# Start addresses of the first layer's moving buffers, chosen per chunk, in a fused attention and feed-forward kernel

## The chip, the core and the metric

The kernel runs on one core of one Trainium2 chip. The metric is the device time of one execution in microseconds (us). Three executions of the kernel before took 633.62, 634.3 and 634.36 us; the median is 634.3 us.

## What is computed

Block-sparse attention is followed by a two-layer feed-forward network. Attention has 4 batches, 8 heads, 768 positions and a head dimension of 64; each query sees its neighbours within 16 positions and one summary of every block of 32 keys. The output becomes a matrix x of 3072 rows by 512 columns, and the network takes it from there:

```python
a = softmax(concat([masked local scores, summary scores + log(32)]))
x = (a @ concat([v, v_sum])).transpose(0, 2, 1, 3).reshape(3072, 512)
h = np.maximum(x @ w_in, 0.0)        # w_in: 512 x 2048
out = (h * h) @ w_out                # w_out: 2048 x 512
```

## The kernel before, in words

The 3072 rows are handled as 24 groups of 128 rows; two groups make a chunk of 256 rows, so there are 12 chunks, numbered 0 to 11. The 2048 hidden columns are 16 slices of 128, called f.

**Two parts for each number.** Every float32 operand of the feed-forward part is split in a high part, rounded to the narrower format that TensorE multiplies in one pass (float32r), and a low part that holds the rest. A product is then three matmuls: high weights by high data, low weights by high data, high weights by low data. For the attention output the two parts are `xh` (written by ScalarE, L375) and `xl` (written by VectorE, L378). For the weights they are `w_sb[f][:, 0]` and `w_sb[f][:, 1]`. For the squared hidden values they are `gh` (L405) and `gl` (L413).

**First layer** (`ffn1`, L387 to L395). For one chunk and one f there are 12 matmuls at L391: for each of 4 slices of the 512 columns the three products above. The weights (128x128) are the stationary operand, loaded anew for each matmul; `xh` or `xl` (128x256) is the moving operand that streams through.

**Second layer** (`ffn2`, L425 to L436). For one chunk and one f there are 6 matmuls at L432. Here `gh` or `gl` (128x128) is the stationary operand and the weights (128x512) are the moving one.

**Order.** The start, chunks 0 and 1, follows a list written out by hand (`START`), while weights are loaded and split. Chunks 2 to 11 then run in a loop over pairs of slices (`slot`): 24 matmuls of the first layer, then the 12 of the second layer for the pair before, and between them the attention work of the chunk after next. A chunk has 8 such slots. At the end of its eighth slot the attention outputs of the next chunk are computed (L361), split into `xh` and `xl`, and the scores of a later one (L278) are taken; TensorE does this between two chunks. All engines take their instructions in the order in which the kernel writes them.

**Buffers.** `x_part` (L368 to L372) hands out the buffer of a chunk: two buffers each for `xh` and `xl`, used in turn, taken from the pool `work`. Each is 4096 bytes long in every partition: 4 slices of 256 float32 numbers, so each slice begins 1024 bytes after the one before. In the program as built all four begin 352 bytes past a multiple of 512. All weights `w_sb` and both `gh` and `gl` begin 160 bytes past a multiple of 512, and the pieces that a matmul takes of them lie at whole multiples of 512 from there. So, counted in bytes modulo 512, the moving operand lies 192 bytes past the stationary one in every matmul of the first layer, and 0 bytes past it in every matmul of the second layer.

Of the kernel before, what the change touches and what calls it, by code (L numbers as in the profile page):

```python
# [12 lines left out]
F32R = mybir.dt.float32r  # L13
# [11 lines left out]
P = 128  # L25
NT = S // P
NPAIR = H // 2
TPC = 2
CT = TPC * P
# [44 lines left out]
def attn_ffn_kernel(ctx: ExitStack, tc: tile.TileContext, q, k, k0, kt, v, vt, v0, w, masks, gmasks, ident, mean, out):  # L74
# [3 lines left out]
    const = ctx.enter_context(tc.tile_pool(name="const", bufs=1))  # L78
    big = ctx.enter_context(tc.tile_pool(name="big", bufs=1))
    work = ctx.enter_context(tc.tile_pool(name="work", bufs=2))  # L80
# [25 lines left out]
    pT = [const.tile([P, H, P], F32, name=f"pT{i}") for i in range(2)]  # L106
    ksum = const.tile([P, NPAIR, NB], F32, name="ksum")
    vsum = const.tile([P, NPAIR, 32], F32, name="vsum")
    r_sb = const.tile([P, 2, CT], F32, name="r")
    gh_sb = const.tile([P, 4, CT], F32R, name="gh")  # L110
    gl_sb = const.tile([P, 4, CT], F32R, name="gl")
# [138 lines left out]
    xh, xl = {}, {}  # L250
# [117 lines left out]
    def x_part(x, name, g):  # L368
        c, o = divmod(g, TPC)
        if c not in x:  # L370
            x[c] = work.tile([P, NPAIR, CT], F32R, name=name, tag=name)
        return x[c][:, :, o * P : (o + 1) * P]  # L372

    def high_x(g):
        nc.scalar.copy(out=x_part(xh, "xh", g), in_=x_ps[g])  # L375

    def low_x(g):
        nc.vector.tensor_sub(out=x_part(xl, "xl", g), in0=x_ps.pop(g), in1=x_part(xh, "xh", g).bitcast(F32))  # L378
# [244 lines left out]
    with tc.manual_schedule(engines=None):  # L623
        for token in START.split():
            what, i, j, eng = re.fullmatch(r"(L:[a-z]+|F[12]|[A-Z]+)\.?(\d*)\.?(\d*)([avp]?)", token).groups()
            i, j = int(i or 0), int(j or 0)
# [10 lines left out]
        for c in range(2, n_c):  # L637
            for f in range(0, NF, 2):
                n = (f + 2) // 2 % 8
# [85 lines left out]
```

## Time and profile before

| what | value |
|---|---|
| median of three executions | 634.3 us (633.62 to 634.36) |
| the profiled execution, its own time | 633.53 us |
| its span, first to last instruction | 631.7 us |
| mean granted TensorE clock | 0.986 |
| TensorE matmuls busy (PE) | 601.6 us, 95% of the span |
| weight loads busy (PEld) | 545.1 us, 86% |
| VectorE (DVE), ScalarE (ACT), GpSimd (POOL) busy | 385.4, 262.5 and 88.8 us |

Such a profile is of one execution. PE is TensorE's matmuls and PEld its weight loads, which overlap them. The recorded duration of one matmul runs from its issue to its modelled end and overlaps that of the next; how fast a stream of matmuls really runs is read from the distance between their starts. The timeline gives, row by row, the start in us, the duration of the merged instructions, the engine, the line, the tiles written and read, and how many were merged.

### The profile page before, as it was taken

Reading aid. Unit: us, or ns where it says so; the run is one execution under the profiler, and the core shown is the slowest. Engines: PE = TensorE matmul, PEld = TensorE weight load, DVE = VectorE, ACT = ScalarE, POOL = GpSimd, SP = SyncE. Lnnn points to the kernel's source line nnn. Section 1 sums busy time; section 2 is a strip of 40 time slices with the busy share of each in tenths; the row PEclk is TensorE's granted clock in tenths of the full one; section 3 lists DMA queues with packets and bytes.
Section 4 is the critical chain, followed back from the end, with each engine's and each line's share of the span. In section 5 each row is a group of like instructions: output and inputs, shape, how many; then the busy total and the mean of one; then the engine's idle time right before and its main releaser. Section 6 shows DMA issues by size and latency. Waiting matters only on the chain.

```text
span 631.7 us, 14142 instructions
## 1 busy us (share of the span) xinstructions
PE 601.6 (95%) x5792; PEld 545.1 (86%) x5792; DVE 385.4 (61%) x1077; ACT 262.5 (42%) x690; POOL 88.8 (14%) x83
## 2 busy tenths in 40 slices
PE   3689999999989999999999998999999999999997
PEld 2588889989979999999989988998998998998996
DVE  4889888668535755756644772783763663653221
ACT  3778887332424324424424423334433423332222
POOL 2555663002000000002000000000200000000000
PEclk9879999999999999999999998999999999999999
DMA  8999611553043134123026115205005001000000
GB/s 290 381 341 317 212 71 52 166 164 90 1 111 110 49 87 132 51 76 93 1 58 162 51 38 148 84 1 135 35 1 135 34 0 52 34 2 1 34 1 33
DMA packets 55104, 60.56 MB, mean 96 GB/s; under 512 B 40320, under 2 KB 40448, under 8 KB 52992
## 3 DMA queue, kind: packets, MB, share of 16 engines
q1 hardware_dynamic: 55040, 59.67, 31.5%
q8 instruction: 45, 0.74, 0.5%
q14 instruction: 19, 0.16, 0.1%
HBM read 53.36 MB, written 6.29 MB: 94 GB/s over the span
## 4 chain that ended last, share of the span: by engine, by line
PE 91%; DMA 4%; DVE 2%; issue 1%; SPq 1%; ACT 0%; DVEq 0%
PE ph L391 41%; PE o_ps L432 41%; DMA w_raw<-in_w 4%; PE ph L361 3%; PE s_ps L391 3%; PE s_ps L278 2%; DVE w_raw L236 1%; PE s_ps L361 1%; PE ph L336 0%; PE s_ps L293 0%; PE s_ps L261 0%; DVE w_sb L247 0%; SPq L171 0%; DVE sm L323 0%; ACT w_raw L225 0%
## 5 line engine op out<-in xcount | busy, mean ns | idle before, releaser
L391 PE MATMUL ph<-xh,w_sb 128*128 128x256 f32 x1448 | 264.2, 284 | 2.8 <-issue 2.2
L391 PEld LDWEIGHTS ph<-xh,w_sb 128*128 128x128 f32 x1448 | 228.9, 190 | 10.7 <-issue 2.4
L432 PE MATMUL o_ps<-w_sb,gh 128*128 128x512 f32 x768 | 237.2, 390 | 0.0
L391 PE MATMUL ph<-xl,w_sb 128*128 128x256 f32 x724 | 204.6, 283 | 0.0
L410 DVE TENSOR_TENSOR ph<-ph,r 128x512 f32<-128x512 f32 (+1 forms) x101 | 64.9, 643 | 160.5 <-ACT r L399 159.2
L432 PEld LDWEIGHTS o_ps<-w_sb,gh 128*128 128x128 f32 x768 | 137.3, 188 | 22.8 <-issue 0.2
L432 PE MATMUL o_ps<-w_sb,gl 128*128 128x512 f32 x384 | 149.7, 390 | 0.9 <-DVE gl L413 0.9
L399 ACT ACTIVATE r<-ph 128x512 f32<-128x512 f32 (+1 forms) x91 | 52.0, 571 | 226.0 <-PE ph L391 225.1
L391 PEld LDWEIGHTS ph<-xl,w_sb 128*128 128x128 f32 x724 | 140.1, 194 | 0.0
L314 ACT ACTIVATE e_sb<-e_sb,nmx 128x88 f32<-128x88 f32 (+1 forms) x192 | 69.9, 367 | 71.3 <-DVE nmx L306 71.3
L347 DVE STREAM_TRANSPOSE pT<-e_sb 32x256 f32<-32x256 f32 x216 | 94.1, 436 | 3.4 <-POOL e_sb L330 0.4
L432 PEld LDWEIGHTS o_ps<-w_sb,gl 128*128 128x128 f32 x384 | 72.1, 188 | 16.4 <-DVE gl L413 1.3
L330 POOL TENSOR_TENSOR e_sb<-e_sb,sm 128x352 f32<-128x352 f32 (+1 forms) x43 | 34.7, 810 | 336.4 <-DVE sm L324 198.4
L413 DVE TENSOR_TENSOR gl<-ph,gh 128x512 fp32r<-128x512 f32 (+1 forms) x101 | 64.3, 637 | 10.5 <-DVE ph L410 0.5
L405 ACT ACTIVATE gh<-r 128x512 fp32r<-128x512 f32 (+1 forms) x112 | 64.0, 571 | 9.3 <-DVE r L401 5.8
L240 POOL TENSOR_TENSOR w_raw<-w_raw 128x1024 int32<-128x1024 int32 x16 | 35.6, 2233 | 25.4 <-DVE w_raw L236 8.7
L314 ACT ACTIVATION_READ_ACCUMULATOR e_sb<-e_sb,nmx 128x1 f32 x192 | 36.4, 190 | 0.0
L306 DVE CUSTOM_DVE_ANT_0 e_sb<-s_ps,gmask_sb 128x88 f32<-128x88 f32 x144 | 27.1, 244 | 0.4
L378 DVE TENSOR_TENSOR xl<-ph,xh 128x512 fp32r<-128x512 f32 x19 | 13.1, 691 | 22.4 <-ACT xh L375 22.4
L323 DVE TENSOR_SCALAR sm<-sm 128x4 f32<-128x4 f32 x48 | 13.4, 280 | 16.0 <-ACT e_sb L314 16.0
L375 ACT CAST xh<-ph 128x512 fp32r<-128x512 f32 x19 | 11.1, 587 | 26.6 <-PE ph L361 26.6
L361 PEld LDWEIGHTS ph<-pT,v_sb 128*64 128x64 f32 x608 | 18.6, 138 | 3.8 <-issue 3.2
(66 smaller groups left out, 391.3 us busy)
## 6 DMA issues: line engine op xcount, KB each, us to landing
w_raw<-in_w SPq DMA_DIRECT2D x16, 1024.0 KB, 14.9
v_sb<-in_v SPq DMA_DIRECT2D x24, 384.0 KB, 4.9
kv<-in_kt SPq DMA_DIRECT2D x16, 384.0 KB, 3.4
q_sb<-in_q SPq DMA_DIRECT2D x24, 256.0 KB, 5.3
out<-ob SPq DMA_DIRECT2D x24, 256.0 KB, 2.1
k_sb<-in_k SPq DMA_DIRECT2D x18, 256.0 KB, 5.1
kv<-in_vt SPq DMA_DIRECT2D x12, 384.0 KB, 3.9
k_sb<-in_k SPq DMA_DIRECT2D x18, 128.0 KB, 5.2
```

Of the source, the lines that this page charges most:

```text
L240: nc.gpsimd.tensor_tensor(out=hi, in0=hi, in1=lo, op=ALU.add)
L306: nc.vector.tensor_tensor_reduce(out=e_sb[:, h, 0:n], in0=s_ps[g][h % 2][:, h // 2, 0:n], in1=m, scale=-scale, scalar=3.0e38, op0=ALU.add, ...
L314: nc.scalar.activation(e, e, AF.Exp, bias=nmx[half][:, i : i + 1], scale=-1.0, accum_out=sm[half][:, i : i + 1])
L330: eng.tensor_mul(out=e, in0=e, in1=sm[half].unsqueeze(2).to_broadcast([P, 4, n]))
L347: nc.vector.transpose(out=pT[g % 2][j * 32 : j * 32 + 32, :, i * 32 : i * 32 + 32], in_=e_sb[i * 32 : i * 32 + 32, :, c : c + 32],)
L361: nc.tensor.matmul(xp[o : o + 64, h // 2, s * 64 : s * 64 + 64], lhsT=v_sb[g % 2][:, s, h * 64 : h * 64 + 64], rhs=pT[g % 2][:, h, s * 64 ...
L391: nc.tensor.matmul(ph, lhsT=w_sb[f][:, w, cc * P : (cc + 1) * P], rhs=x[c][:, cc, :], start=(n == 0), stop=(n == 3 * NC4 - 1))
L399: nc.scalar.activation(r, ph, AF.Relu)
L405: nc.scalar.activation(gh, r, AF.Square)
L410: nc.vector.tensor_mul(out=ph, in0=ph, in1=r)
L413: nc.vector.tensor_sub(out=gl, in0=ph, in1=gh.bitcast(F32))
L432: nc.tensor.matmul(o_ps[c][tt], lhsT=g_[:, ts_], rhs=w_sb[f][:, w, DM:], start=(first and n == 0), stop=(last and n == 2),)
```

## The change

The buffers of `xh` and `xl` are no longer taken from the pool. Four buffers (two for each, used in turn as before) are allocated once, 512 bytes longer than needed. For each chunk a table gives where in its buffer `xh` and `xl` begin, in bytes:

```diff
+    begin_x = [(0, 0), (0, 0), (0, 0), (64, 64), (128, 128), (192, 192), (256, 256), (32, 32), (0, 64), (0, 128), (0, 256), (320, 320)]
+    x_buf = {n: [const.tile([P, NPAIR * CT + 128], F32R, name=f"{n}{i}") for i in range(2)] for n in ("xh", "xl")}
...
         if c not in x:
-            x[c] = work.tile([P, NPAIR, CT], F32R, name=name, tag=name)
+            o_ = begin_x[c % len(begin_x)][0 if name == "xh" else 1] // 4
+            x[c] = x_buf[name][c % 2][:, o_ : o_ + NPAIR * CT].rearrange("p (a k) -> p a k", a=NPAIR)
         return x[c][:, :, o * P : (o + 1) * P]
```

In the program as built the new buffers begin 160 bytes past a multiple of 512, as the weights do, so the table's numbers are the distances of the moving operand from the weights, modulo 512. Before, that distance was 192 in every chunk; now it is 0 in chunks 0 to 2, 192 in chunk 5 alone, and another number in each of the others; in chunks 8 to 10 `xh` is at 0 and `xl` at 64, 128 and 256. The buffers of `r`, `gh`, `gl` and the weights lie 18432 bytes (36 times 512) further on than before, so their places modulo 512, and with them the second layer's distance of 0, are as they were. The instructions of every engine, their order and the semaphore values that they wait for are the same in both programs; the addresses alone differ.

## The prediction

> **What bounds the kernel now.** I read the page of the profile first: the busy times, then the chain that ended last.
>
> ```profile
> PE 601.6 (95%) x5792; PEld 545.1 (86%) x5792; DVE 385.4 (61%) x1077; ACT 262.5 (42%) x690; POOL 88.8 (14%) x83
> PE 91%; DMA 4%; DVE 2%; issue 1%; SPq 1%; ACT 0%; DVEq 0%
> L391 PE MATMUL ph<-xh,w_sb 128*128 128x256 f32 x1448 | 264.2, 284 | 2.8 <-issue 2.2
> L391 PE MATMUL ph<-xl,w_sb 128*128 128x256 f32 x724 | 204.6, 283 | 0.0
> L432 PE MATMUL o_ps<-w_sb,gh 128*128 128x512 f32 x768 | 237.2, 390 | 0.0
> ```
>
> TensorE's matmuls hold 91% of the chain, and the two lines that matter, L391 (first layer) and L432 (second layer), wait for almost nothing: 2.8 us before 1448 matmuls. So the kernel's time is the distance between the starts of successive matmuls, summed. No engine's order changes here; what can change is that distance. I therefore read the timeline, matmuls alone, at two places. The first is a slot in the middle of a chunk:
>
> ```profile
> 297.76 0.40 PE L391 MATMUL ph<-xh,w_sb 128*128 128x256 f32 x2
> 298.00 0.28 PE L391 MATMUL ph<-xl,w_sb 128*128 128x256 f32 x1
> ...
> 300.59 0.62 PE L432 MATMUL o_ps<-w_sb,gh 128*128 128x512 f32 x2
> ...
> 303.31 0.40 PE L391 MATMUL ph<-xh,w_sb 128*128 128x256 f32 x2
> ```
>
> The 24 first-layer matmuls take 300.59 - 297.76 = 2.83 us, 117.9 ns each; the 12 second-layer ones take 303.31 - 300.59 = 2.72 us, 226.7 ns each. A second-layer matmul streams 512 columns, a first-layer one 256. At the second layer's pace 256 columns would take 113.3 ns. So the first layer loses 4.6 ns in each matmul against a pace that the same engine keeps right behind it.
>
> The second place is the first slot of a chunk, just after TensorE did the attention work:
>
> ```profile
> 430.97 0.50 PE L391 MATMUL ph<-xh,w_sb 128*128 128x256 f32 x2
> 431.31 0.28 PE L391 MATMUL ph<-xl,w_sb 128*128 128x256 f32 x1
> 431.43 0.39 PE L391 MATMUL ph<-xh,w_sb 128*128 128x256 f32 x2
> ...
> 433.81 0.63 PE L432 MATMUL o_ps<-w_sb,gh 128*128 128x512 f32 x2
> 434.27 0.39 PE L432 MATMUL o_ps<-w_sb,gl 128*128 128x512 f32 x1
> 434.51 0.62 PE L432 MATMUL o_ps<-w_sb,gh 128*128 128x512 f32 x2
> ...
> 436.55 0.40 PE L391 MATMUL ph<-xh,w_sb 128*128 128x256 f32 x2
> ```
>
> From 431.43 to 433.81 stand 21 first-layer matmuls: 2.38 us, 113.3 ns each. Same operands, same addresses modulo 512, same instructions as in the other slot, and 4.6 ns less. So 113.3 ns is reachable, and 117.9 is a stall that depends on how weight reads and moving reads happen to stand to each other. And the phase that suits the first layer here does not suit the second: the first three second-layer matmuls take 434.51 - 433.81 = 0.70 us, 233 ns each, before the rest settle to 226.7 (436.55 - 434.51 = 2.04 us for 9). After that the next first-layer matmuls are back at 118.
>
> How common each state is, the recorded times tell. First the groups of the two slots (297.7 to 300.6 us, then 432.3 to 433.75), with the mean of one in ns last; then the view of line L391 over the whole run (minimum, median, maximum), with the weight loads beside it:
>
> ```profile
> L391 PE MATMUL ph<-xh,w_sb 128*128 128x256 f32 x16 | 2.9, 281 | 0.0
> ...
> L391 PE MATMUL ph<-xh,w_sb 128*128 128x256 f32 x10 | 1.7, 276 | 0.0
> ...
> L391 PE MATMUL ph<-xh,w_sb x1448: 276/281/580, 36.8 to 622.4; 128*128 128x256 f32 x181
> L391 PEld LDWEIGHTS ph<-xl,w_sb x724: 187/192/330, 37.2 to 622.4; 128*128 128x128 f32 x181
> L432 PEld LDWEIGHTS o_ps<-w_sb,gh 128*128 128x128 f32 x8 | 1.4, 188 | 0.2
> ```
>
> The minimum of 276 goes with the quick slot and the median of 281 with the slow one: the slow state is the usual one. The weight loads show it too: those for the `xl` products have a median of 192 ns where the quickest take 187, and those under the second layer (third row, the same slot from 300.62 to 303.2) take 188.
>
> My reading: in the stream that TensorE settles into, a distance of 0 bytes between moving and stationary operand (second layer) costs no stall, a distance of 192 (first layer) costs 4.6 ns.
>
> **The change, part by part.** Removed: nothing that runs. Added: nothing. Moved: where `xh` and `xl` lie. ScalarE and VectorE write them and TensorE reads them, at other addresses. The writes cost as before (same instructions, off the chain: ACT holds 0% of it and is 42% busy). What is left is the first layer's distance between starts, chunk by chunk.
>
> *Distance 0: chunks 0 to 2, and the `xh` products of chunks 8 to 10.* The nearest row is the second layer's at the same distance, which runs without the stall; the far bound is the 117.9 of now. I take 113.3, since the first layer starts from the phase in which the second layer leaves it, and its weight load then meets the moving stream at the same addresses modulo 512 as it did in the second layer.
>
> - Chunk 2: seven of its eight slots run slow now (the first after the attention work is quick in part, and pays some of it back in the second layer). 7 x 24 x 4.6 ns = 0.77 us.
> - Chunks 8 to 10: two of three products have the distance 0: 3 x 0.77 x 2/3 = 1.54 us.
> - Chunks 0 and 1: the chain in order of time, and the stage of the start in which TensorE runs without a break:
>
> ```profile
> 99.35 2.83 PE ph L391 x24
> 115.99 2.83 PE ph L391 x24
> 139.97 2.94 PE ph L391 x24
> 95.00:131.00 36.00, 22.02 (x179) 21.90 (x179) 1.00 0.37 111
> ```
>
> (The third row is the first slot of chunk 2.) Between 95 and 131 us 179 first-layer matmuls run at 2.83 us per 24, and nothing but TensorE ends there: 179 x 4.6 ns = 0.82 us. Before 95 us the start waits for weights and their splitting, so I count nothing; the upper bound is all 384 matmuls of the two chunks, 1.77 us.
>
> *Distance 192: chunk 5.* As now: 0.
>
> *Distances 32, 64, 128, 256, 320: chunks 7, 3, 4, 6, 11, and the `xl` products of chunks 8 to 10.* No row shows any of them. The bounds from both sides: all free of the stall, 0.77 us per chunk gained; or a stall once more as large, 0.77 us per chunk lost. I take the nearest measured distance: 128, 256 and 320 lie nearer to 192 than 0 does, so nothing; 32 and 64 lie between 0 and 128, nearer to 0, and I count half of 0.77 for each of the two chunks, 0.77 together. For the `xl` products nothing.
>
> Sum: 0.77 + 1.54 + 0.82 + 0.77 = 3.9 us off the profiled execution's 633.53. The profiled execution lies 0.8 under the median, and I take the same 3.9 off the median: 634.3 - 3.9 = **630.4 us**.
>
> What hides nothing but can blur it: in one stage the granted clock falls.
>
> ```profile
> 381.28 4.57 PE ph L391 x24
> 431.04 2.93 PE ph L391 x24
> ```
>
> The first slot after 381 us takes 4.57 us where its like at 431 takes 2.93: 1.6 us, in a stretch of half clock behind the attention work. With a slightly other timing it can stay away or come twice; it belongs to no term and widens the range.
>
> A rule of the Trainium skill speaks against all of this. "SBUF — State Buffer", section "Who interferes with whom", gives TensorE two read ports that are independent of each other, one for the moving operand and one for weight loads, and says that it never waits on anyone; "TensorE: Matmul & The Clock Gate", Part 2, says that loading the next weights takes no read bandwidth from the running matmul. By that the place of a buffer could change nothing, and the sum would be 634.3; the two states of 113.3 and 117.9 at equal operands do not agree with it, as far as I read them as stalls on reads.
>
> **The rivals.**
>
> *No change (the stall is not one of addresses).* The stall of 4.6 ns may come from the hand-over alone: a first-layer matmul lasts about as long as a weight load, a second-layer one twice as long, so only the first layer would suffer when load and matmul wait for each other in turn. Then every distance gives 117.9 and the time is 634.3. For it: only the layer with short matmuls shows the stall, at one distance, so distance and length are not told apart by this trace. Against it: the 233 ns of second-layer matmuls behind a quick slot, where the weight load has half of the matmul's time to spare, so that a hand-over should cost nothing.
>
> *Slower: 0 is the worst distance, and the second layer only hides it.* Weight load and moving stream begin together and then ask for the same places at the same time. In the second layer a load delayed by this still ends long before its matmul. In the first layer it does not, and each matmul waits for its load. The price: the only delay seen at distance 0 is 233 - 226.7 = 6 ns; on top of 117.9 this is 6 ns for each matmul at distance 0. Chunk 2: 192 x 6 ns = 1.15 us; chunks 8 to 10: 2.3; the start: 179 x 6 ns = 1.07; together 4.5, and 638.8 us. For it: nothing measures a short matmul at distance 0. Against it: weight loads at distance 0 are recorded at 188 ns, not longer than in the quick state. It decides as soon as the starts in chunk 2 lie further apart than 118 ns.
>
> *Every new distance is free and 192 alone collides.* Nine chunks gain 0.77, and the start up to 1.77: 634.3 - 8.7 = 625.6 us. For it: a collision wants a certain distance, and most may miss it. Against it: behind each attention stop the stream needs several matmuls to find the quick pace (431.43 - 430.97 = 0.46 us for the first three), so collisions are not rare.
>
> **How the numbers follow.** The forecast, with its neighbours up to all distances free: 0.55. No change: 0.25. Slower, by distance 0 or by the unmeasured distances colliding harder (five chunks and a third of three, 6 x 0.77 = 4.6 us, against the 3.1 gained at distance 0: 635.8): 0.20. A measurement of this kernel tells about 0.2%, 1.3 us, from no change. The range starts at 626.0, near the all-free case, and ends at 636.5, past the case of harder collisions with 0.7 us for the spread of the executions; it leaves out most of the rival at 638.8 and a second clock drop on top. Chances: faster 0.55, within 0.2% 0.25, slower 0.20. If it is faster, I expect 626 to 632.5.
>
> **What the profile after would show.** Chunk 2 (from 140 us on in the profile before): slots of 24 first-layer matmuls in 2.72 us instead of 2.83, recorded time 276 ns; the second layer still 2.72 for 12, with no 233 behind the first slot. Chunk 5: still 2.83. Chunks 8 to 10: 2.75 to 2.76. If chunk 2 stays at 2.83, the step from the second layer's distance to the first layer's is wrong, and the no-change rival holds; if it is over 2.83, the slower one does. The chunks 3, 4, 6, 7 and 11 tell the unmeasured distances directly, each by its own slots.

## The result and the profile after

The changed kernel is slower: a median of 637.41 us in 11 executions, against 633.66 us for 11 of the kernel before. The ratio taken over the runs is 1.0065, with a 95% interval of 1.0043 to 1.0087 (the two medians alone give 1.0059). The forecast was 630.4, with a range from 626.0 to 636.5.

The page of the profile after has the same shape as before: TensorE on the chain, next to no waiting.

```profile
span 634.6 us, 14142 instructions
PE 605.5 (95%) x5792; PEld 546.8 (86%) x5792; DVE 386.1 (61%) x1077; ACT 262.7 (41%) x690; POOL 88.3 (14%) x83
PE 93%; DMA 3%; DVE 2%; issue 1%; SPq 0%; ACT 0%; DVEq 0%
L395 PE MATMUL ph<-xh,w_sb 128*128 128x256 f32 x1448 | 265.3, 283 | 2.6 <-issue 2.1
```

So it is again the distance between starts that counts. The chain in order of time shows whole slots, merged: start, duration, and 24 matmuls of the first layer (now L395) or 12 of the second (L436). Here is one of each, in order for chunks 2, 3, 4, 5 and 7. Before the change such a row inside a chunk read 2.83 and 2.72.

```profile
151.58 2.87 PE ph L395 x24
154.45 2.75 PE o_ps L436 x12
...
199.79 2.76 PE o_ps L436 x12
202.55 2.83 PE ph L395 x24
...
248.27 2.76 PE o_ps L436 x12
251.04 2.88 PE ph L395 x24
...
296.99 2.72 PE o_ps L436 x12
299.71 2.83 PE ph L395 x24
...
396.44 2.80 PE ph L395 x24
```

Chunk 2, at distance 0, takes 2.87 where 2.72 was forecast; chunk 5, still at 192, takes 2.83 and 2.72 as before. The table has one slot (24 first-layer and 12 second-layer matmuls, the middle one of five slots inside the chunk, from the starts in the trace) for every chunk:

| chunk | distance of xh, xl | first layer, us | second layer, us | together | against 5.547 |
|---|---|---|---|---|---|
| 2 | 0, 0 | 2.872 | 2.748 | 5.620 | +0.073 |
| 3 | 64, 64 | 2.830 | 2.757 | 5.587 | +0.040 |
| 4 | 128, 128 | 2.875 | 2.765 | 5.640 | +0.093 |
| 5 | 192, 192 | 2.827 | 2.720 | 5.547 | 0 |
| 6 | 256, 256 | 2.873 | 2.747 | 5.620 | +0.073 |
| 7 | 32, 32 | 2.802 | 2.744 | 5.546 | 0 |
| 8 | 0, 64 | 2.827 | 2.746 | 5.573 | +0.026 |
| 9 | 0, 128 | 2.827 | 2.719 | 5.546 | 0 |
| 10 | 0, 256 | 2.872 | 2.748 | 5.620 | +0.073 |
| 11 | 320, 320 | 2.830 | 2.757 | 5.587 | +0.040 |

The last column sums to 0.42 us; times 8 slots it is 3.3 us. The stage of the start from about 95 to 131 us grew by 0.76 us (36.92 against 36.16, of which 0.26 is one interruption), after a beginning that was 0.6 us quicker. Table and start together make 3.5 us; the medians differ by 3.75 and the profiled spans by 2.9. The 0.6 us by which the spans fall short lies mostly between chunks: TensorE's stretch of attention work before chunk 10 took 3.82 us in the profile after and 4.37 in the one before. The stretch of lower clock that the prediction named stands in both profiles, near 382 and 384 us, so it isn't the difference. So the loss is where the table puts it, spread over seven chunks and the start, and both layers have a share (0.25 of the 0.42 us is the second layer's), although no address of the second layer's matmuls changed modulo 512.

How a slot of chunk 2 loses it, the timeline of its matmuls shows:

```profile
151.41 0.40 PE L395 MATMUL ph<-xh,w_sb 128*128 128x256 f32 x2
151.65 0.28 PE L395 MATMUL ph<-xl,w_sb 128*128 128x256 f32 x1
151.77 0.40 PE L395 MATMUL ph<-xh,w_sb 128*128 128x256 f32 x2
...
154.29 0.63 PE L436 MATMUL o_ps<-w_sb,gh 128*128 128x512 f32 x2
154.76 0.39 PE L436 MATMUL o_ps<-w_sb,gl 128*128 128x512 f32 x1
154.99 0.62 PE L436 MATMUL o_ps<-w_sb,gh 128*128 128x512 f32 x2
155.45 0.39 PE L436 MATMUL o_ps<-w_sb,gl 128*128 128x512 f32 x1
155.68 0.61 PE L436 MATMUL o_ps<-w_sb,gh 128*128 128x512 f32 x2
```

From the third row on 21 first-layer matmuls take 154.29 - 151.77 = 2.52 us, 120 ns each, a third state beside the 113.3 and 117.9 of before. The single starts of such a slot are 113, 119, 120, 120, 120 ns apart, and 120 from there on: the first matmul does run at the quick pace that was forecast, then the stream slides into a stall and stays. And the second layer pays for the phase in which it is left: its first six matmuls take 155.68 - 154.29 = 1.39 us, 232 ns each, before it is back at 226.7.

Distance alone doesn't settle the pace. Chunk 4, at distance 128, has the slowest slots of the table, 120 ns a matmul in the mean. But its first slot, entered from the attention work and not from the second layer, runs in the quick state:

```profile
234.47 0.39 PE L395 MATMUL ph<-xh,w_sb 128*128 128x256 f32 x2
...
236.85 0.63 PE L436 MATMUL o_ps<-w_sb,gh 128*128 128x512 f32 x2
```

These are 21 first-layer matmuls in 2.38 us, 113.3 ns each, at a distance that gives 120 in all its later slots.

### The profile page after: what moved, and what is told of

Its sections match the earlier page's. It is cut to its first block, busy times and chain, and to the rows that moved or that the text cites. A ratio compares the mean times of both kernels' runs of the same rounds, so it can differ in the third digit from the quotient of the medians.

```text
span 634.6 us, 14142 instructions
## 1 busy us (share of the span) xinstructions
PE 605.5 (95%) x5792; PEld 546.8 (86%) x5792; DVE 386.1 (61%) x1077; ACT 262.7 (41%) x690; POOL 88.3 (14%) x83
## 4 chain that ended last, share of the span: by engine, by line
PE 93%; DMA 3%; DVE 2%; issue 1%; SPq 0%; ACT 0%; DVEq 0%
PE ph L395 41%; PE o_ps L436 41%; PE ph L364 3%; PE s_ps L395 3%; PE s_ps L281 2%; DMA q_sb<-in_q 2%; PE s_ps L296 1%; DMA mask_sb<-in_masks 1%; DVE e_sb L309 1%; PE s_ps L364 1%; PE ph L339 1%; PE s_ps L264 0%; DVE sm L326 0%; SPq L174 0%; DVE w_raw L239 0%
## 5 line engine op out<-in xcount | busy, mean ns | idle before, releaser
L395 PE MATMUL ph<-xh,w_sb 128*128 128x256 f32 x1448 | 265.3, 283 | 2.6 <-issue 2.1
L395 PEld LDWEIGHTS ph<-xh,w_sb 128*128 128x128 f32 x1448 | 230.0, 191 | 10.8 <-issue 2.6
L436 PE MATMUL o_ps<-w_sb,gh 128*128 128x512 f32 x768 | 238.8, 392 | 0.0
L395 PE MATMUL ph<-xl,w_sb 128*128 128x256 f32 x724 | 204.5, 282 | 0.0
L436 PEld LDWEIGHTS o_ps<-w_sb,gh 128*128 128x128 f32 x768 | 137.6, 188 | 23.8 <-issue 0.2
L436 PE MATMUL o_ps<-w_sb,gl 128*128 128x512 f32 x384 | 150.0, 390 | 0.8 <-DVE gl L417 0.8
L395 PEld LDWEIGHTS ph<-xl,w_sb 128*128 128x128 f32 x724 | 138.1, 191 | 0.0
L436 PEld LDWEIGHTS o_ps<-w_sb,gl 128*128 128x128 f32 x384 | 72.1, 188 | 17.3 <-DVE gl L417 1.3
```

The lines of the kernel that those rows point to most:

```text
L395: nc.tensor.matmul(ph, lhsT=w_sb[f][:, w, cc * P : (cc + 1) * P], rhs=x[c][:, cc, :], start=(n == 0), stop=(n == 3 * NC4 - 1))
L436: nc.tensor.matmul(o_ps[c][tt], lhsT=g_[:, ts_], rhs=w_sb[f][:, w, DM:], start=(first and n == 0), stop=(last and n == 2),)
```

## The experiments

Theory D, formed from this table: the pace of a stream of matmuls depends on the distance between what streams and what is loaded at the same time, and on the phase that the matmuls before have left. Its rivals were that the new places of the buffers cost the time (L), later that the absolute place of the moving operand does (A), and that a stall settles only where the weight load has no time to spare.

**e1: the new buffers, the old distance.**

```diff
-    begin_x = [(0, 0), (0, 0), (0, 0), (64, 64), ... (320, 320)]
+    begin_x = [(192, 192)] * 12
```

> The changed kernel with distance 192 in every chunk: the new buffers and all addresses moved as in the change, but the old distance. Theory D (the distance between moving operand and weights sets the pace): slots of 2.83 us for 24 first-layer matmuls and 2.72 for 12 second-layer ones in all chunks as before the change, 633.7 us, no difference to before. Rival L (what costs is where the buffers now lie, the 18432 bytes by which weights and gh, gl moved and the moving operand lying ahead of them): 636 to 637.5, slots as slow as in the changed kernel's mean.

Measured: 633.48 us in 12 executions against 633.21 of the kernel before; ratio 1.0015, interval 0.9995 to 1.0034. All ten chunks took 2.827 and 2.720 us per slot in the middle, here chunk 5:

```profile
292.52 2.83 PE ph L395 x24
295.34 2.72 PE o_ps L436 x12
```

Rival L falls: moving weights, `gh` and `gl` by 18432 bytes and placing the moving buffers ahead of them costs nothing that can be told. The numbers in the table alone made the change slower.

**e2: distance 0 everywhere.**

```diff
+    begin_x = [(0, 0)] * 12
```

> Distance 0 in every chunk. Theory D: every slot as in chunk 2 of the changed kernel, 2.87 + 2.75 us against 2.83 + 2.72, 0.07 us more in each of 80 slots = 5.6 us, and up to 0.5 us in the start: 639 to 640 us. Rival L: 636 to 637.5, as the changed kernel. The slower rival of the prediction, with its price of 6 ns for each first-layer matmul: 2304 x 6 ns = 13.8 us, 647.

Measured: 638.96 us in 6 executions, ratio 1.0102, interval 1.0057 to 1.0146. Every chunk repeats chunk 2 of the changed kernel; a slot of chunk 5 on the chain:

```profile
290.11 2.87 PE ph L395 x24
292.99 2.75 PE o_ps L436 x12
```

The distance that the prediction took for free is slower than the old one, in whatever chunk. The price is 0.045 us per 24 first-layer matmuls (1.9 ns each) and 0.028 us per 12 second-layer ones, 5.8 us in 80 slots, where theory D had 5.6; not the 6 ns for each first-layer matmul of the prediction's rival.

**e3 and e5: more distances, one per chunk.** Both kernels keep chunks 0 and 1 at 192.

```diff
+    begin_x = [(192, 192)] * 2 + [(v, v) for v in (16, 48, 96, 160, 224, 80, 112, 8, 4, 384)]
+    begin_x = [(192, 192)] * 2 + [(v, v) for v in (100, 104, 108, 116, 120, 124, 144, 176, 240, 368)]
```

> Chunks 2 to 11 at distances 16, 48, 96, 160, 224, 80, 112, 8, 4 and 384, read slot by slot. Theory D with a period of 256 bytes: 384 gives 2.88 + 2.77 as 128 did. If a stall is one of whole lines of 32 or 64 bytes, 4, 8 and 16 give what 0 gives (2.87 + 2.75); if single words count, they differ. 160 and 224, either side of 192, 2.80 to 2.85. Rival (no period under 512): 384 gives something else than 128. No sum for the whole kernel is forecast.

> Chunks 2 to 11 at distances 100, 104, 108, 116, 120, 124, 144, 176, 240 and 368, read slot by slot; 24 first-layer and 12 second-layer matmuls together took 5.547 us at 192 and 5.506 at 112. Theory D with a period of 256: 368 gives 5.506 as 112 did, 240 something else. If there is a period of 128 instead, 240 gives 5.506 too. If the phase that the second layer leaves has to be met within a few bytes, 108 and 116 differ from 112; if within a line of 16 bytes, 112, 116, 120 and 124 agree.

Measured, both layers of a slot together, in us (5.547 at 192):

| distance | slot | distance | slot | distance | slot |
|---|---|---|---|---|---|
| 4 | 5.713 | 100 | 5.633 | 144 | 5.520 |
| 8 | 5.627 | 104 | 5.826 | 160 | 5.580 |
| 16 | 5.580 | 108 | 5.607 | 176 | 5.620 |
| 48 | 5.607 | 112 | 5.506 | 224 | 5.607 |
| 80 | 5.606 | 116 | 5.674 | 240 | 5.573 |
| 96 | 5.647 | 120 | 5.640 | 368 | 5.506 |
| | | 124 | 5.547 | 384 | 5.640 |

368 repeats 112, 384 repeats 128, as in the change 256 repeated 0 and 320 repeated 64: four pairs, all equal, so here a period of 256 bytes is enough, and 240 against 112 excludes one of 128. Within it there is no smooth course: 104 and 112 lie 8 bytes apart and are the slowest and the quickest of all. Nor is it a matter of whole lines of 16, 32 or 64 bytes: 4, 8 and 16 give 5.713, 5.627 and 5.580 where 0 gave 5.620, and 112 to 124 don't agree. The guess of 2.80 to 2.85 us for the first layer on either side of 192 held at 224 (2.839) and just missed at 160 (2.854). Forecasting a distance from its neighbours, as the prediction did for 32, 64, 128, 256 and 320, has no ground. The kernels took 637.24 and 640.21 us in one execution each, which says nothing beyond the slots.

**e4: distances of their own for xh and xl.**

```diff
+    begin_x = [(192, 192)] * 2 + [(192, 0), (192, 64), (192, 32), (192, 128), (64, 192), (32, 192), (128, 192), (0, 192), (64, 128), (32, 128)]
```

> Chunks 2 to 11 with xh and xl at distances of their own: (192,0), (192,64), (192,32), (192,128), (64,192), (32,192), (128,192), (0,192), (64,128), (32,128). If each product stalls by its own distance alone, the first-layer slot is two thirds of the xh distance's time and one third of the xl distance's: (192,0) 2.84, (192,32) 2.82, (0,192) 2.86, (32,192) 2.81, (32,128) 2.83. If the phase is carried from matmul to matmul, as (0,128) at 2.83 and (0,64) at 2.83 in the changed kernel suggest (2.87 and 2.86 by that rule), it is something else, and a pair could be quicker than 2.80.

Measured (637.25 us in one execution): the first layer's part was 2.825, 2.828, 2.859, 2.847, 2.827, 2.837, 2.827, 2.827, 2.825 and 2.827 us. The rule of thirds fails: (32,192) was to be 2.81 and took 2.837, (192,32) was to be 2.82 and took 2.859. No pair was quicker than 2.80, so that hope failed too. What fits, but isn't shown by itself, is that a matmul's delay shifts the phase for the next.

**e6: everything else moved instead.** 192 bytes of nothing ahead of `r`, `gh`, `gl` and the weights, and a table of beginnings that gives the distances named below:

```diff
+    const.tile([P, 48], F32, name="gap")
     r_sb = const.tile([P, 2, CT], F32, name="r")
```

> Weights, gh and gl moved on by 192 bytes to 352 past a multiple of 512, moving operands of chunks 2 to 11 at distances 0, 64, 128, 192, 32, 112, 16, 48, 80 and 4 from them, modulo 256. Theory D (distance alone): slots as measured with the weights at 160: 5.620, 5.587, 5.640, 5.547, 5.546, 5.506, 5.580, 5.607, 5.606, 5.713 us. Rival A (the absolute place of the moving operand decides): each slot as the one whose absolute place it shares, that is distance 192 more: 5.547 for 0, 5.620 for 64, 5.587 for 128, 5.640 for 192.

Measured (637.34 us in one execution): 5.620, 5.587, 5.640, 5.547, 5.546, 5.506, 5.580, 5.607, 5.606 and 5.713 us, the ten numbers of theory D, to within 0.001 us. Chunk 7 of it, at 112, on the chain (its lines are L396 and L437):

```profile
396.03 2.76 PE ph L396 x24
398.79 2.75 PE o_ps L437 x12
```

Rival A falls: moved by 192 bytes together, the operands keep their pace at all ten distances, so it is not the place of the moving operand by itself but its distance from the weights that matters.

**e7: the second layer's distance.** `gh` and `gl` get longer buffers too, and begin elsewhere in each chunk; the first layer stays at 192.

```diff
+    begin_g = [0, 0, 32, 64, 96, 128, 160, 192, 224, 112, 16, 48]
...
     def slot(c, f, before, after, last):
+        nonlocal gh_sb, gl_sb
+        gh_sb, gl_sb = g_at(begin_g[c])
```

> First layer at distance 192 throughout; gh and gl, the second layer's stationary operands, moved by 32, 64, 96, 128, 160, 192, 224, 112, 16 and 48 bytes in chunks 2 to 11 (its distance was 0). Theory D with slack (a second-layer weight load has half of its matmul's time to spare, so it steps aside once and no longer stalls): the settled second-layer matmul stays at 226.7 ns at every distance, and only the first few of a slot, and with them the phase handed to the first layer, change; slots between 5.50 and 5.65 us. Rival (0 is a lucky distance for the second layer): settled second-layer matmuls over 226.7 ns at some distances, a slot longer by up to 12 x 4.6 ns = 0.055 us.

Measured (637.54 us in one execution, the slots in the middle of the chunks between 5.493 and 5.631): the settled second-layer matmuls were 226.7 ns apart at none of the ten places; nine distances gave 231 to 233 ns in the mean of a slot, and 192, the best, 229. So the rival holds: 0, where the second layer lay by chance, is the best of its eleven distances, and time to spare in the load does not protect it at the others. But five of the ten places (32, 48, 112, 160 and 192) put the first layer, at its old distance, in the quick state of 113.3 ns in every settled slot, after a few slower matmuls. Three (16, 64 and 128) did so in every second slot, and 96 and 224 in none once the chunk had settled. Chunk 3, at 64, has the two by turns:

```profile
209.29 2.74 PE ph L400 x24
...
214.82 2.83 PE ph L400 x24
```

Chunk 7, with `gh` and `gl` moved by 192, took 5.493 us:

```profile
397.68 2.75 PE ph L400 x24
400.42 2.75 PE o_ps L441 x12
```

The second layer gives up 0.028 us, the first gains 0.081. The same first-layer operands at the same distance run at 117.8 or at 113.3 ns, by what ran before them: the phase is carried.

**e8: that place in all chunks.**

```diff
+    begin_x = [(192, 192)] * 12
+    begin_g = [(192, 192)] * 12
```

> First layer at distance 192 as before the change, gh and gl moved by 192 bytes in every chunk (the slot that took 5.493 us in chunk 7 of the sweep of gh and gl). Theory D, with the phase carried from one layer to the other: every slot 5.49 us against 5.547, 80 x 0.054 = 4.3 us less, and up to 0.5 in the start: 628.5 to 629.5 us, quicker than both kernels. Rival (the quick slot of chunk 7 was a phase that one chunk happened to be in): slots of several lengths over the chunks and 631 to 634 us.

Measured: 627.51 us in 12 executions against 633.17 of the kernel before; ratio 0.9913, interval 0.9883 to 0.9943. That is quicker than forecast, and quicker than the kernel before, which the change had made slower. All ten chunks took 2.746 and 2.748 us (a slot of chunk 5):

```profile
290.51 2.75 PE ph L400 x24
293.26 2.75 PE o_ps L441 x12
```

80 slots x 0.054 us are 4.3 of the 5.7 us, and the start is 0.5 us shorter in the profile. In its profiled execution the clock also stayed up where it dropped in the kernel before: the first slot behind the attention work near 380 us took 2.94 us, against 4.57 before, 1.6 us. These are the granted clock before, then that of e8 and its slot:

```profile
PEclk9879999999999999999999998999999999999999
...
PEclk9979999999999999999999999999999999999999
378.84 2.94 PE ph L400 x24
```

How much of the median the clock makes was not measured.

**e9: both layers' distances together** (`s(v)` stands for `(v, v)`).

```diff
+    begin_x = [s(192)]*2 + [s(112), s(144), s(32), s(192), s(192), s(112), s(144), s(192), s(192), s(144)]
+    begin_g = [s(0)]*2 + [s(192), s(192), s(192), (0, 192), (192, 0), s(16), s(112), (0, 16), (0, 112), s(64)]
```

> Moving operands at distance (112, 144, 32, 192, 192, 112, 144, 192, 192, 144) and gh, gl moved by ((192,192), (192,192), (192,192), (0,192), (192,0), (16,16), (112,112), (0,16), (0,112), (64,64)) in chunks 2 to 11, read slot by slot. If the two layers only add up, 112 with 192 gives the first layer's 2.76 and the second's 2.75; if the phase is carried, neither is kept, and slots lie between 5.44 (no stall at all: 24 x 113.3 + 12 x 226.7) and 5.65 us with no rule that one could have named.

Measured (634.59 us in one execution): 5.526, 5.555, 5.574, 5.514, 5.527, 5.500, 5.640, 5.527, 5.546 and 5.640 us; chunks 3 and 11 switch from slot to slot (5.555 and 5.591, 5.640 and 5.653). The layers don't add up: 112 is the first layer's best distance and `gh`, `gl` at 192 the best second place, but the two together took 2.773 + 2.753 = 5.526 instead of 2.76 + 2.75, worse than that place with 192 (5.493). None came near 5.440, the time without any stall, and none beat e8.

**e10: half the weight load.** Each first-layer load and matmul takes 64 of the 128 hidden columns, so half of the first layer is left out; the 256 columns stream as before.

```diff
-                    ph, lhsT=w_sb[f][:, w, cc * P : (cc + 1) * P], rhs=x[c][:, cc, :], ...
+                    ph[0:64], lhsT=w_sb[f][:, w, cc * P : cc * P + 64], rhs=x[c][:, cc, :], ...
```

> Leaves out half of the first layer: each weight load and matmul takes 64 of the 128 hidden columns, so a load lasts half as long while its matmul streams 256 columns as before. Distances 0, 64, 128, 192, 32, 112, 16, 48, 80 and 4 in chunks 2 to 11. Theory D with slack (a first-layer matmul settles in a stall because its load has no time to spare): the first layer settles at 113.3 ns or near it at most distances, 24 matmuls in 2.72 to 2.76 us. Rival (reads collide whether or not the load has time to spare): slots over 2.76 at several distances, in a pattern by distance, as gh and gl's distances showed for the second layer (230 to 234 ns).

Measured (632.68 us in one execution): 24 first-layer matmuls took 2.728 us at distance 0, and 2.802, 2.802, 2.850, 2.851, 2.803, 2.828, 2.836, 2.819 and 2.876 at 64, 128, 192, 32, 112, 16, 48, 80 and 4. The recorded time of a load fell from a median of 188 ns (the kernel before, first row) to 134 (e10):

```profile
L391 PEld LDWEIGHTS ph<-xh,w_sb x1448: 186/188/333, 36.8 to 622.3; 128*128 128x128 f32 x181
...
L395 PEld LDWEIGHTS ph<-xh,w_sb x1448: 132/134/227, 35.2 to 621.4; 128*64 128x64 f32 x181
```

Half of the columns are 54 ns less, so by an estimate from these two rows a whole load takes about 108 ns beyond a fixed part, nearly all of a first-layer matmul's 113 ns, and a half one 54. At nine of ten distances a stall stays all the same. So the rival holds again: a load with time to spare is not enough to be free of the stall, and the hand-over between load and matmul can't be the whole cause. Yet at distance 0 the half load does what the prediction expected of the whole one (chunk 2):

```profile
153.00 2.73 PE ph L395 x24
155.73 2.74 PE o_ps L436 x12
```

## Why the prediction was wrong, point by point

*What bounds the kernel, and the two states.* Right. The distance between starts carried the difference, the 113.3 ns is reachable (e7, e8), and the state is a matter of phase and place.

*"A distance of 0 bytes costs no stall", carried over from the second layer to the first.* This is the step that failed. It was true of the second layer, and true of the first layer's first matmul (113 ns), but from the second one on the stream slid into a stall of 120 ns. The second layer's distance 0 says nothing of the first layer's: with half the weight load, as long against its matmul as the second layer's, distance 0 is free (2.728 us), with the whole load it is not (2.872). The argument compared two streams at equal addresses and took the different length of load and matmul for harmless. So, by the table, chunk 2 lost 0.6 us instead of gaining 0.77; chunks 8 to 10 lost 0.8 instead of gaining 1.54, and the stage of the start lost 0.5 (0.76 with the interruption) instead of gaining 0.82.

*The unmeasured distances.* The bounds of 0.77 us either way held for all five chunks (0 to +0.093 us per slot, at most 0.75 in a chunk). Taking the nearest measured distance failed: 32 gave nothing, 64 lost 0.3, and 128, 256 and 320, counted at nothing, lost 0.7, 0.6 and 0.3. Two of its readings were loose besides: 64 lies midway between 0 and 128, not nearer to 0, and 256 is, by the period found later, distance 0 once more.

*What stayed uncounted.* The second layer. The profile before showed the second layer paying for the phase of the quick slot (233 ns three times); the prediction noted it and expected it to be gone, but put no term for the second layer into its sum. It lost 0.02 to 0.045 us per slot in eight of ten chunks, together 0.25 of the table's 0.42 us.

*The rivals.* No change: refuted, since slots of one kernel ran from 5.546 to 5.640 us by distance alone. "0 is the worst distance, and the second layer only hides it": the right sign and the right chunks at 638.8 us, with a price three times too high (1.9 ns for 6) and the second layer and the other distances left out, which made up for it, so that it came near the measured 637.41 is luck; and 0 is not the worst (4, 104 and 128 among others are worse). Its mechanism, a load that is delayed and has no time to spare, fits distance 0 with the whole and the half load (e10), but leaves open why the stall stays at the other nine. The loads at 188 ns that spoke against it were the second layer's: in the first layer at distance 0 the loads have a median of 192 (e2). Its chance of 0.20 was too low: the trace had two distances to compare in layers of different shape, which is no measurement of a short matmul at distance 0, as the rival itself said. "Every new distance is free and 192 alone collides": refuted too, since no new distance of the change held the first layer at 113.3 ns; in the settled slots 32 alone came under the old 117.8, with 116.7.

*The rule of the Trainium skill* ("SBUF — State Buffer", section "Who interferes with whom") has the two read ports of TensorE independent, from which the prediction inferred that the place of a buffer could change nothing: the runs disagree with what it inferred, with slots between 5.493 and 5.826 us by distance alone. What is behind it is not settled. That the delay hangs on the distance between what streams and what is loaded, modulo 256 bytes, is shown, and so is that the matmuls before have a part in it; that it is two reads meeting in the same part of memory is argued only, since no row shows a read.

## What to carry to other kernels

Where TensorE is the bound and weights are reloaded for each matmul, read the distance between starts, not the recorded duration, and compare it between layers and behind stops: two paces for the same operands mean that buffer places are worth trying. Don't derive the best place from one layer for another or from its neighbours; give one candidate to each repeat of a loop, read ten of them from one profile, and then time the best in all repeats. Judge a place by the time of all layers that follow each other, since a stall left by one is paid by the next.

## What the runs showed of the hardware

- The time of a slot repeats with the distance modulo 256 bytes (0 and 256, 64 and 320, 112 and 368, 128 and 384 agree), and, away from the stops, it is the same within 0.001 us in all chunks of a kernel that uses one distance (e1, e2 and e8; one chunk of e1 needed two slots to get there).
- Steps of 4 and 8 bytes matter: 5.674 us at 116, 5.506 at 112, 5.826 at 104.
- Most streams settle within some ten matmuls in one of several paces and keep it: 113.3, 116.7 (distance 32), 117.8 or 120 ns for 256 columns, and others that repeat every three matmuls (118, 120, 122 at 128) or two (123, 137 at 104). Which one it is depends on what ran before as well: at 128, 113.3 behind the attention work and 120 behind the second layer; at 192, 117.8 or 113.3 by the second layer's place.
